# First-stage folds on VectorE in the front, and a new order of products and loads in odd steps

## The chip, the cores and the metric

The kernel runs on one core of a Trainium2 chip. The metric is the device time of one execution in microseconds (us). Before the change three timed runs gave 871.84, 869.36 and 871.62 us, median 871.62.

## What is computed

Two stages in one launch. The first is a causal long convolution by Fourier transform: x has 8 batches of 5696 tokens of 128 features, h is one filter of the same length for each feature. The second is a soft mixture of experts over all 45568 tokens: 32 slots, 8 experts.

```python
L = 2 * S                                  # S = 5696
Xf = np.fft.rfft(x, n=L, axis=1); Hf = np.fft.rfft(h, n=L, axis=0)
y = np.fft.irfft(Xf * Hf[None], n=L, axis=1)[:, :S, :]
x = y.reshape(B * S, D)
logits = x @ phi
d = softmax(logits, over tokens); slot_input = d.T @ x
slot_out[e] = relu(slot_input[e] @ w1[e]) @ w2[e]
c = softmax(logits, over slots); out = c @ slot_out
```

All data are float32.

## The kernel before

The transform is split in two factors, N1 = 90 and N2 = 64, and is done by matrix products with tables. There are nine groups of sequences: group 0 is h, groups 1 to 8 are the batches of x. The work is a pipeline of three parts.

- **A, the first stage.** A group is cut into NJ = 8 chunks, so there are NA = 72. `load_x(c)` (L184) fetches chunk c in two DMAs into one of three buffers xc. `fold(c, comp)` (L201, operation at L206) makes the sum (comp 0) and the difference (comp 1) of a chunk's two halves, the second half read backwards; each is one GpSimd operation of 128 x 512. The results lie in four buffers `xf`, two for even and two for odd chunks. `first_stage` (L210) multiplies them with the table s1 (L217), evicts two PSUM banks on ScalarE (L220) into a tile `fst` (four buffers) and stores that into f in DRAM (L226). `first_low(c)` makes the first 64 rows of the transform of one chunk; `first_high(c)`, in odd steps alone, makes the last 32 rows for the two chunks c-1 and c at once, and so reads all four `xf` buffers.
- **B, the spectrum.** `load_g` (L253) brings f back in twelve units per group (99 loads of 512 KB and 9 of 128 KB in all); `stage_b1` multiplies (L267) and, on VectorE, builds the filter's spectrum for group 0 (L285, L289) or multiplies with it (L285, L294); `stage_b2` transforms back (L309, evicted at L315) and stores into z in DRAM (L318).
- **C, the tokens.** `load_pair` (L346) brings z back into one buffer zc. `stage_c1` makes the last products (L365), with sums and differences on VectorE (L370, L371) and GpSimd (L384); `stage_c2` transposes (L393), `stage_c3` makes the logits (L402), `stage_c4`, `c5`, `softmax`, `dispatch` and `stage_c6` make both softmaxes and the running sum of slot inputs.

The order is written out by hand: the scheduler is switched off, and every engine works through its instructions in program order. A loop over steps t runs one letter after another of a string, `ORDER_E` when t is odd and `ORDER_O` when it is even (L577):

```python
ORDER_E, ORDER_O, XAHEAD = "xXYf1wb5s", "zPxXfb26db3m", 3
```

"x" is load_x(t + 3), "X" first_low(t), "Y" first_high(t), "f" both folds of chunk t + 1, "1" stage_c1 with stage_c4 in its middle, "w" what is left of stage_c1, "b" one unit of B, "z" load_pair, "P" load_g for the steps ahead. Part B lags by LAG_B = 9 steps, part C by 27. So steps 0 to 8 hold part A alone. All loads and stores of the loop are issued by SyncE (SP), one queue, in this same order: a load or store that has to wait holds up all behind it. After the loop comes a tail with its own order: the last token tiles, the experts (L767 to L788) and the output (L822 to L833).

Of the kernel before, what the change touches and what calls it, by code (L numbers as in the profile page):

```python
# [12 lines left out]
AL = mybir.AluOpType  # L13
# [64 lines left out]
def kernel(  # L78
# [24 lines left out]
    nc = tc.nc  # L103
# [3 lines left out]
    E, _, F = moe_w1.shape  # L107
# [16 lines left out]
    QP = HP // 2  # L124
# [18 lines left out]
    NT = B * NQ  # L143
# [52 lines left out]
                out=t_[X0 + r.start:X0 + r.stop, :, :, :].rearrange("p s n d -> p s (n d)"), in_=v)  # L196
        xs[c] = t_

    folded = {}

    def fold(c, comp):  # L201
        if c not in xs:
            return
        t_ = xs.pop(c) if comp else xs[c]
        y_ = xf[c % 2 * 2 + comp]
        nc.gpsimd.tensor_tensor(out=y_[:, :, :], in0=t_[:, 0, :, :], in1=t_[:, 1, ::-1, :],  # L206
                                op=AL.subtract if comp else AL.add)
        folded[(c, comp)] = y_

    def first_stage(tiles, width):  # L210

        st = apool.tile([P, CH, 2, D], F32, name="fst", tag="fst", bufs=4)
        for G in range(2):
            p = bank()
            for o, (c, comp) in enumerate(tiles):
                k = slice(0, HP) if width == HP else slice(HP, HP + QP)
                nc.tensor.matmul(p[o * width:(o + 1) * width, :], s1[:, comp + G, k],  # L217
                                 folded[(c, comp)][:, :, :].rearrange("p n d -> p (n d)"),
                                 start=True, stop=True)
            nc.scalar.activation(st[:, :, G, :],  # L220
                                 p[:, :].rearrange("p (n d) -> p n d", d=D), AF.Copy)
        for o, (c, comp) in enumerate(tiles):
            g, j = divmod(c, NJ)
            n0 = comp * HALF + CH * j
            k0, n = (0, N1A) if width == HP else (N1A, N1 - N1A)
            nc.sync.dma_start(  # L226
                out=fd[g].rearrange("q a r c d -> (q a) (r c d)")[k0:k0 + n, n0 * 2 * D:(n0 + CH) * 2 * D],
                in_=st[o * width:o * width + n, :, :, :].rearrange("k n c d -> k (n c d)"))
# [2 lines left out]
        first_stage([(c, comp) for comp in range(2)], HP)  # L231

    def first_high(c):

        both = [(c - 1 + i, comp) for i in range(2) for comp in range(2)]
        first_stage(both, QP)
        for b_ in both:
            del folded[b_]

    gs, prods = {}, {}  # L240

# [107 lines left out]
                                    a=2)[r:r + n, j * w_:(j + 1) * w_])  # L349
        zs[T] = t_  # L350

    def stage_c1(T, between):
        t_ = zs.pop(T)
        kr = used if t_ is zn else P
        y_ = ybufs.pop(0)
        ybufs.append(y_)

        def part(v, f):
            k = (2 * v + f) * CH
            return y_[:, k:k + CH, 0:D] if f == 0 else y_[:, k + CH - 1:k - 1:-1, 0:D]  # L360

        def product(o, tab, q):
            p = bank()
            for h_ in range(2):
                nc.tensor.matmul(p[h_ * HP:(h_ + 1) * HP, :], i1[0:kr, tab, :],  # L365
                                 t_[0:kr, h_, o, :, q, :], start=True, stop=True)
            return p[:, :].rearrange("p (n d) -> p n d", d=D)

        def fold_out(even, minus, plus):
            nc.vector.tensor_tensor(out=plus, in0=even, in1=minus, op=AL.add)  # L370
            nc.vector.tensor_tensor(out=minus, in0=even, in1=minus, op=AL.subtract)  # L371

        b_, a_ = product(0, 1, 1), product(0, 0, 0)
        nc.scalar.activation(part(0, 0), b_, AF.Copy)
        fold_out(a_, part(0, 0), part(1, 0))
        between()
        b_, a_ = product(1, 1, 0), product(1, 2, 1)
        nc.scalar.activation(om[:, :, :], b_, AF.Copy)

        def after():  # L380
            fold_out(a_, om[:, :, :], op[:, :, :])
            for v, o_, eng in ((1, op, nc.gpsimd), (0, om, nc.vector if tail else nc.gpsimd)):
                for part_, sign in ((part(v, 1), AL.subtract), (part(v, 0), AL.add)):
                    eng.tensor_tensor(out=part_, in0=part(v, 0), in1=o_[:, :, :], op=sign)  # L384

        ys[T] = y_
        return after

    def stage_c2(T):
        for k in (3, 1, 0, 2) if tail else (3, 2, 1, 0):  # L390
# [183 lines left out]
    for comp in range(2):  # L574
        fold(0, comp)
    wait_b2 = []
    ORDER_E, ORDER_O, XAHEAD = "xXYf1wb5s", "zPxXfb26db3m", 3  # L577

    for t in range(last_front + 1):
        us = list(units(t))  # L580

        def pair(lag):
            T, half = divmod(t - LAG_C - lag, 2)
            return T if half == 0 and 0 <= T < NT else None

        def prefetch(last):
            nonlocal loaded
            while loaded < len(queue) and queue[loaded][1] <= last:
                load_g(queue[loaded][0])
                loaded += 1  # L590

        def slot_b():
            fresh = bool(us)
            if fresh:
                u = us.pop(0)
                stage_b1(u, t < LAG_C or t >= NA)
                wait_b2.append(u)
            if len(wait_b2) > fresh:
                stage_b2(wait_b2.pop(0))

        T, U = pair(0), pair(2)
        after = []
        work_ = {
            "z": lambda: load_pair(pair(-1)) if pair(-1) is not None else None,
            "x": lambda: load_x(t + XAHEAD) if t < NA else None,
            "p": lambda: prefetch(t + 1) if t % NJ else None,
            "P": lambda: prefetch(t + 2),
            "q": lambda: prefetch(t + 1),
            "X": lambda: first_low(t) if t < NA else None,
            "Y": lambda: first_high(t) if t < NA and t % 2 else None,  # L610
            "f": lambda: [fold(t + 1, comp) for comp in range(2)] if t < NA else None,
            "d": lambda: dispatch(pair(3)) if pair(3) is not None else None,
            "b": lambda: slot_b(),
            "1": lambda: after.append(stage_c1(T, lambda: stage_c4(U) if U is not None else None))
            if T is not None else stage_c4(U) if U is not None else None,
            "w": lambda: [a_() for a_ in after],
            "2": lambda: stage_c2(pair(1)) if pair(1) is not None else None,
            "6": lambda: stage_c6(pair(5)) if pair(5) is not None else None,
            "5": lambda: stage_c5(U) if U is not None else None,
            "3": lambda: stage_c3(pair(1)) if pair(1) is not None else None,  # L620
            "m": lambda: column_max(pair(1)) if pair(1) is not None else None,
            "s": lambda: softmax(U) if U is not None else None,
            "g": lambda: prefetch(t + 1) if t % NJ == 0 else None,
        }
        if t == last_front:
            if pair(-1) is not None:
                load_pair(pair(-1))
            assert T is None and U is None
            if pair(3) is not None:
                dispatch(pair(3))  # L630
            slot_b()
            slot_b()
            slot_b()
            stage_c2(pair(1))
            slot_b()
            assert not us and not wait_b2
            V = pair(1)
            stage_c6(V - 2)
            stage_c3(V)
            column_max(V)  # L640
            break
        for c_ in (ORDER_E if t % 2 else ORDER_O):
            work_[c_]()
        assert not us
        if t == NA:
            lead.close()
            wts = inner.enter_context(tc.tile_pool(name="wts", bufs=1, side="right"))
            w1s = wts.tile([P, E, F], F32, name="w1s")
        if NA < t <= NA + E:
            nc.sync.dma_start(out=w1s[:, t - NA - 1, :], in_=moe_w1[t - NA - 1])  # L650
# [19 lines left out]
    tail["pool"] = cload.enter_context(tc.tile_pool(name="cload", bufs=2))  # L670
    y_ = tail["pool"].tile([P, Q * CH, D + 1], F32, name="y2", tag="y2", bufs=1)

    after = stage_c1(T, lambda: stage_c4(V))
    after()
    stage_c5(V)
    softmax(V)
    nc.gpsimd.memset(y_[:, :, D:D + 1], 1.0)
# [21 lines left out]
    for V in range(T, NT):  # L699
# [10 lines left out]
        N = T + 1 if V == T else V + 2  # L710
        after = None
        if N < NT:
            after = stage_c1(N, lambda: stage_c4(V))
            load_pair(N + 2)
        else:
            stage_c4(V)
        if after:
            after()
        if V > T:
            placed_c()  # L720
        stage_c5(V)
# [3 lines left out]
        softmax(V)  # L725
        if V == T:
            ybufs.insert(0, y_)
            stage_c1(T + 2, lambda: None)()
            load_pair(T + 4)
        else:  # L730
            for i in range(4 * (V - T - 1), min(4 * (V - T), E), 2):
                nc.sync.dma_start(
                    out=w2s[:, i:i + 2, :, :],
                    in_=moe_w2[i:i + 2].rearrange("e (p c) d -> p e c d", p=P))
    stage_c6(NT - 2)
    assert list(Ls) == [NT - 1] and not (ys or ds or prods or gs or zs or xs or folded or wait_b2
                or kept or landed)


# [129 lines left out]
```

## Time and profile before

| what | value |
|---|---|
| median of three runs | 871.62 us |
| the profiled execution's own time | 869.17 us |
| its span, first to last instruction | 867.4 us |
| granted TensorE clock, mean | 0.954 |
| TensorE busy (PE) | 770.7 us, 89% |
| VectorE busy (DVE) | 619.2 us, 71% |
| GpSimd busy (POOL) | 403.7 us, 47% |
| ScalarE busy (ACT) | 441.6 us, 51% |
| moved by DMA | 272.46 MB, mean 314 GB/s |
| folds, L206, on GpSimd | 144 of 1274 ns |

How to read the lines of the profile that follow. A group's line has the source line, the engine, the operation, the tiles as out<-in, and how many. In a timeline a line begins with the start and the length in us; the bracket at its end has the idle time of the engine ahead of it and what ended that. In the chain of waits a line has the start, the length and what the chain ran through. "SPq" is SP's queue of DMA issues. A stretch is a window of the span; its columns are the busy time of PE, PEld (weight loads, beside PE), DVE, ACT and POOL with counts, the granted clock, the mean busy share of the 16 DMA engines, and GB/s. A TensorE matmul of this kernel appears as two records, so the four matmuls of a low product appear as x8, the eight of a high product as x16.

### The profile page before, as it was taken

The numbers are of one execution on the slowest core, as the hardware profiler recorded it, in microseconds if no ns is written. First come the engines' busy times: TensorE is split into PE (matmuls) and PEld (weight loads), VectorE is DVE, ScalarE is ACT, GpSimd is POOL, SyncE is SP. The second block draws the span as 40 slices with busy tenths as digits, with TensorE's granted clock in tenths as the row PEclk, the third lists the DMA queues.
The fourth block names the chain that finished last, engine by engine and source line by source line (L and its number), as shares of the span: only waits on it lengthen the run. The fifth ranks groups of instructions, "written<-read, shape, count | busy, mean of one in ns | idle before, by whom it ended". The sixth has DMA issues, their size and how long they took to land.

```text
span 867.4 us, 20489 instructions
## 1 busy us (share of the span) xinstructions
PE 770.7 (89%) x7796; PEld 376.2 (43%) x7796; DVE 619.2 (71%) x928; ACT 441.6 (51%) x904; POOL 403.7 (47%) x385
## 2 busy tenths in 40 slices
PE   5888888888999999999999999999988879977893
PEld 1122333234444444444444444444444444444882
DVE  3059967667777878877888788877789995953552
ACT  2433344344555565556566556655544445773541
POOL 4453433245565555656555655556434432671000
PEclk9999999999999999999999999999999898989865
DMA  9899899999999999999999999999998986580898
GB/s 294 272 296 310 296 333 342 332 332 334 339 315 321 340 324 329 347 329 345 338 339 337 338 338 339 346 327 343 320 314 283 320 301 247 219 305 2 335 405 341
DMA packets 156109, 272.46 MB, mean 314 GB/s; under 512 B 12183, under 2 KB 113687, under 8 KB 152870
## 3 DMA queue, kind: packets, MB, share of 16 engines
q1 hardware_dynamic: 155435, 270.85, 90.2%
q8 instruction: 62, 1.02, 0.5%
q10 hardware_dynamic: 576, 0.31, 0.1%
q14 instruction: 36, 0.29, 0.1%
HBM read 142.81 MB, written 128.21 MB: 312 GB/s over the span
## 4 chain that ended last, share of the span: by engine, by line
PE 60%; DMA 15%; DVE 11%; SPq 3%; issue 2%; POOL 1%; ACT 1%; DVEq 0%; ACTq 0%
PE bank L217 14%; PE bank L365 13%; PE bank L309 7%; PE bt L267 7%; PE bank L393 6%; DMA zc<-z 6%; DMA out_dram<-o 3%; PE bank L478 3%; DVE yf L294 2%; DVE p L285 2%; DVE bt L285 2%; SPq L346 2%; DMA gt<-f 2%; PE op L822 2%; PE bank L402 2%
## 5 line engine op out<-in xcount | busy, mean ns | idle before, releaser
L206 POOL TENSOR_TENSOR x<-xc 128x512 f32<-128x512 f32 x144 | 180.0, 1274 | 229.5 <-PE bank L217 208.6
L217 PE MATMUL bank<-x,s 128*32 128x512 f32 (+1 forms) x1152 | 227.7, 613 | 16.0 <-DMA xc<-in_h_dram 8.1
L315 ACT ACTIVATE zst<-bank 128x512 f32<-128x512 f32 (+1 forms) x184 | 98.6, 586 | 190.9 <-PE bank L309 173.9
L220 ACT ACTIVATE fst<-bank 128x512 f32<-128x512 f32 x216 | 127.4, 598 | 109.5 <-PE bank L217 93.5
L285 DVE TENSOR_TENSOR p<-bt,Hi 128x1024 f32<-128x1024 f32 x96 | 111.4, 1160 | 33.7 <-PE bt L267 32.8
L309 PE MATMUL bank<-yf,vt 64*64 64x256 f32 x1440 | 103.1, 392 | 27.5 <-DVE yf L294 27.5
L365 PE MATMUL bank<-zc,i 128*64 128x512 f32 x480 | 115.8, 604 | 12.1 <-DMA zc<-z 8.2
L217 PEld LDWEIGHTS bank<-x,s 128*32 128x32 f32 (+1 forms) x1152 | 56.1, 124 | 155.5 <-issue 76.2
L294 DVE TENSOR_TENSOR yf<-bt,p 128x512 f32<-128x512 f32 x192 | 119.4, 663 | 3.3
L267 PE MATMUL bt<-gt,wt 64*64 64x256 f32 x1620 | 113.7, 388 | 5.8 <-DVE Hi L289 2.4
L285 DVE TENSOR_TENSOR bt<-bt,Hr 128x1024 f32<-128x1024 f32 x96 | 113.0, 1177 | 0.0
L267 PEld LDWEIGHTS bt<-gt,wt 64*64 64x64 f32 x1620 | 54.0, 132 | 80.6 <-issue 36.7
L309 PEld LDWEIGHTS bank<-yf,vt 64*64 64x64 f32 x1440 | 57.2, 136 | 58.9 <-issue 27.8
L384 POOL TENSOR_TENSOR y<-y,op 128x512 f32<-128x512 f32 x64 | 77.9, 1217 | 8.3 <-DVE op L370 5.2
L370 DVE TENSOR_TENSOR y<-bank,y 128x512 f32<-128x512 f32 x32 | 22.1, 691 | 72.8 <-PE bank L365 72.6
L393 PE MATMUL bank<-ident,y 109*128 109x109 f32 x512 | 64.3, 278 | 0.7 <-DVE y L384 0.7
L384 POOL TENSOR_TENSOR y<-y,om 128x512 f32<-128x512 f32 x54 | 64.0, 1185 | 2.1
L365 PEld LDWEIGHTS bank<-zc,i 128*64 128x64 f32 x480 | 30.5, 136 | 74.8 <-issue 47.1
L393 PEld LDWEIGHTS bank<-ident,y 109*128 109x128 f32 x512 | 54.3, 151 | 16.7 <-issue 11.1
L395 ACT ACTIVATE yt<-bank 128x360 f32<-128x360 f32 x128 | 51.4, 492 | 3.1 <-PE bank L393 3.1
L439 POOL MEMSET dt<- 64x8 f32 x32 | 3.4, 106 | 104.8 <-issue 70.7
L822 PE MATMUL op<-so,cT 32*128 32x128 f32 x704 | 45.6, 368 | 4.7 <-ACT o L831 4.3
(97 smaller groups left out, 824.6 us busy)
## 6 DMA issues: line engine op xcount, KB each, us to landing
gt<-f SPq DMA_DIRECT2D x99, 512.0 KB
z<-zst SPq DMA_DIRECT2D x88, 512.0 KB
f<-fst SPq DMA_DIRECT2D x144, 240.0 KB
zc<-z SPq DMA_DIRECT2D x30, 1024.0 KB
xc<-in_x_dram SPq DMA_DIRECT2D x64, 320.0 KB
f<-fst SPq DMA_DIRECT2D x144, 120.0 KB
out_dram<-o SPq DMA_DIRECT2D x16, 1024.0 KB
zc<-z SPq DMA_DIRECT2D x90, 128.0 KB
```

The source lines that it names most:

```text
L206: nc.gpsimd.tensor_tensor(out=y_[:, :, :], in0=t_[:, 0, :, :], in1=t_[:, 1, ::-1, :], op=AL.subtract if comp else AL.add)
L217: nc.tensor.matmul(p[o * width:(o + 1) * width, :], s1[:, comp + G, k], folded[(c, comp)][:, :, :].rearrange("p n d -> p (n d)"), start=Tr ...
L220: nc.scalar.activation(st[:, :, G, :], p[:, :].rearrange("p (n d) -> p n d", d=D), AF.Copy)
L267: nc.tensor.matmul(bt[q * HP:(q + 1) * HP, a, o, :], wt[r, 2 * i + q, :], t_[r, 2 * o + q, :, :].rearrange("p c d -> p (c d)"), start=True ...
L285: nc.vector.tensor_tensor(out=p_, in0=pv, in1=h_, op=AL.mult)
L294: eng.tensor_tensor(out=y_[r, 0:k, c, :], in0=pv[:, :, c, :], in1=pi[r, 0:k, 1 - c, :], op=op_)
L309: nc.tensor.matmul(bz[q][a * HP:(a + 1) * HP, o * 2 * D:(o + 1) * 2 * D], vt[r, i, a, :], y_[r, a * m + o, :, :].rearrange("p c d -> p (c ...
L315: nc.scalar.activation(st[:, 0:m, q, :], bz[q][:, 0:m * 2 * D].rearrange("p (o x) -> p o x", o=m), AF.Copy)
L365: nc.tensor.matmul(p[h_ * HP:(h_ + 1) * HP, :], i1[0:kr, tab, :], t_[0:kr, h_, o, :, q, :], start=True, stop=True)
L384: eng.tensor_tensor(out=part_, in0=part(v, 0), in1=o_[:, :, :], op=sign)
L393: nc.tensor.transpose(p[:, i * TR:(i + 1) * TR], ys[T][0:TR, k * CH + i, 0:D], ident[0:TR, 0:TR])
L822: nc.tensor.matmul(pq[q][:, k * D:(k + 1) * D], cT[rows, b, r0:r0 + RW, :] if k < n else cL[rows, :, :], so4[rows, :], start=True, stop=True)
```

## The change

Four edits, three of which alter what runs when.

1. The folds of the chunks 0 to 8 (c < LAG_B), which are those made ahead of the first B unit, go to VectorE. The others stay on GpSimd.
2. In odd steps the high product ("Y") comes first, then the folds of the next chunk ("f"), and then the low product ("X").
3. In odd steps the loads of x ("x") are issued after the stores of both products, not ahead of them.
4. `stage_c1` becomes a generator whose three pieces are "1", "j" and "w", with stage_c4 as a letter "4" of its own. The pieces come in the same order as before. `folded` becomes a function in place of a dictionary, which alters no instruction.

Even steps are as before.

```diff
-    folded = {}
+    def folded(c, comp):
+        return xf[c % 2 * 2 + comp]
...
         t_ = xs.pop(c) if comp else xs[c]
-        y_ = xf[c % 2 * 2 + comp]
-        nc.gpsimd.tensor_tensor(out=y_[:, :, :], in0=t_[:, 0, :, :], in1=t_[:, 1, ::-1, :],
-                                op=AL.subtract if comp else AL.add)
-        folded[(c, comp)] = y_
+        eng = nc.vector if c < LAG_B else nc.gpsimd
+        eng.tensor_tensor(out=folded(c, comp)[:, :, :], in0=t_[:, 0, :, :],
+                          in1=t_[:, 1, ::-1, :], op=AL.subtract if comp else AL.add)
...
-    def stage_c1(T, between):
+    def stage_c1(T):
...
         fold_out(a_, part(0, 0), part(1, 0))
-        between()
+        yield
         b_, a_ = product(1, 1, 0), product(1, 2, 1)
...
         ys[T] = y_
-        return after
+        yield
+        after()
+        yield
...
-    ORDER_E, ORDER_O, XAHEAD = "xXYf1wb5s", "zPxXfb26db3m", 3
+    ORDER_E, ORDER_O, XAHEAD = "YfXx14jwb5s", "zPxXfb26db3m", 3
...
-            "1": lambda: after.append(stage_c1(T, lambda: stage_c4(U) if U is not None else None))
-            if T is not None else stage_c4(U) if U is not None else None,
-            "w": lambda: [a_() for a_ in after],
+            "1": lambda: next(c1, None),
+            "4": lambda: stage_c4(U) if U is not None else None,
+            "j": lambda: next(c1, None),
+            "w": lambda: next(c1, None),
```

More of the change, by code (lines that the diff above doesn't have):

```diff
@@ L217, in first_stage @@
                 nc.tensor.matmul(p[o * width:(o + 1) * width, :], s1[:, comp + G, k],
-                                 folded[(c, comp)][:, :, :].rearrange("p n d -> p (n d)"),
+                                 folded(c, comp)[:, :, :].rearrange("p n d -> p (n d)"),
                                  start=True, stop=True)
@@ L233, in first_high @@
     def first_high(c):
[L235 to L238, printed above, removed]
+        first_stage([(c - 1 + i, comp) for i in range(2) for comp in range(2)], QP)
     gs, prods = {}, {}
@@ L601 @@
         T, U = pair(0), pair(2)
-        after = []
+        c1 = stage_c1(T) if T is not None else iter(())
         work_ = {
@@ L671 @@
     y_ = tail["pool"].tile([P, Q * CH, D + 1], F32, name="y2", tag="y2", bufs=1)
-    after = stage_c1(T, lambda: stage_c4(V))
-    after()
+    after = stage_c1(T)
+    next(after)
+    stage_c4(V)
+    next(after)
+    next(after)
     stage_c5(V)
@@ L712 @@
         if N < NT:
-            after = stage_c1(N, lambda: stage_c4(V))
+            after = stage_c1(N)
+            next(after)
+            stage_c4(V)
+            next(after)
             load_pair(N + 2)
@@ L717 @@
         if after:
-            after()
+            next(after)
         if V > T:
@@ L727 @@
             ybufs.insert(0, y_)
-            stage_c1(T + 2, lambda: None)()
+            for _ in stage_c1(T + 2):
+                pass
             load_pair(T + 4)
@@ L735 @@
     stage_c6(NT - 2)
-    assert list(Ls) == [NT - 1] and not (ys or ds or prods or gs or zs or xs or folded or wait_b2
+    assert list(Ls) == [NT - 1] and not (ys or ds or prods or gs or zs or xs or wait_b2
                 or kept or landed)
```

## The prediction

> **What bounds the kernel now.** I read the busy row by slices first, then the front of the kernel by stretches, then its timeline, and last the waits and the steady loop.
>
> The page shows three regimes. Each digit is the busy share of a fortieth of the span (21.7 us).
>
> ```profile
> PE   5888888888999999999999999999988879977893
> DVE  3059967667777878877888788877789995953552
> DMA  9899899999999999999999999999998986580898
> ```
>
> From slice 10 to 29 the tensor engine and the DMA engines are both at nine tenths or more: there, no rearrangement gains much. In the first two slices VectorE stands at 3 and 0, and DMA falls to 8. So the front has room. The stretch view cuts it at the pairs of first-stage steps (columns: PE, PEld, DVE, ACT, POOL busy, granted clock, DMA share, GB/s).
>
> ```profile
> 17.65:26.56 8.91, 7.17 (x33) 1.75 (x33) 0.00 (x0) 3.58 (x6) 4.95 (x5) 1.00 0.94 332
> 26.56:35.44 8.88, 7.15 (x33) 1.74 (x33) 0.00 (x0) 3.58 (x6) 4.92 (x5) 1.00 0.88 274
> 35.44:44.32 8.88, 7.15 (x33) 1.74 (x33) 0.00 (x0) 3.58 (x6) 4.92 (x5) 1.00 0.84 257
> 44.32:53.20 8.88, 8.17 (x48) 2.25 (x48) 0.34 (x1) 3.58 (x6) 4.92 (x5) 1.00 0.87 263
> ```
>
> A pair of steps takes 8.88 us there and nothing is full. The timeline says what sets that period.
>
> ```profile
> 25.24 4.92 POOL L206 TENSOR_TENSOR x<-xc 128x512 f32<-128x512 f32 x4 [3.96 <-PE bank L217]
> 26.56 7.45 PE L217 MATMUL bank<-x,s 128*64 128x512 f32 x32 [1.43 <-POOL x L206]
> ```
>
> It is a ring of two engines. GpSimd makes four folds (4.92 us) and then waits 3.96 us for the high product, because that is the last reader of the four fold buffers; TensorE in turn waits for the folds. 4.92 + 3.96 = 8.88: the period exactly. VectorE has no work in it at all (its first product comes at 52.86 us after 43.35 us idle).
>
> In the steady loop the same fold wait costs nothing. The chain of waits there is TensorE laid end to end; one pair of steps from 500.50 to 520.76 is 20.26 us, and 17 pairs from 234.34 to 581.10 average 20.40.
>
> ```profile
> 500.50 3.72 PE bank L217 x24
> 504.22 1.87 PE bank L365 x8
> ...
> 520.76 3.72 PE bank L217 x24
> ```
>
> [...] the trace has 691 ns for the sums of L370. [...] here 1274 ns (L206) over 691 is 1.84. [...] L384 on VectorE, both inputs in SBUF, takes 711 ns at best but 1552 ns in the median, beside L384 on GpSimd. [...] a load put behind a store in SP's queue inherits the store's wait. The trace shows such waits: SP before L226 for ACT fst, 14.0 us over 18.
>
> **The change part by part.**
>
> *Folds of chunks 0 to 8 on VectorE.* Eighteen folds leave GpSimd and go to VectorE; in the built program's instruction order they stand behind VectorE's start-up fills and ahead of its first product of the spectrum. Price of one: no such op (two SBUF inputs, GpSimd idle) is in the trace; the bounds are 0.69 (L370) and 1.55 us (L384 beside GpSimd). GpSimd has nothing else in the front, so I take 0.71, L384's minimum. Per pair: 4 x 0.71 = 2.8 us instead of 4.92. At the upper bound 4 x 1.55 = 6.2, still under 8.88.
>
> *The start.* VectorE fills zc, lt, dt and y until 9.6 us (zc 3.47 us from 4.89), where GpSimd folds from 6.83. So the first product moves from 8.15 to about 9.6 + 0.7 = 10.3: 2.2 us later. I cost it at nothing, because DMA is at 0.99 from 2.00 to 17.65 us, moving tables that the later stages need; if that cover is gone it costs up to 2.2.
>
> *High product first in odd steps.* The 24 matmuls stay 24 (3.72 us in the steady loop: 1.87 for the low ones, 1.85 for the high ones). But the even buffers come free after the high product, and the next even fold runs under the low one. The ring then is: high product, [fold | low product], [next fold | low product of the even step]. Each fold pair, 1.42 us, lies under a product of 1.87. The ring becomes TensorE's own 3.72 + 1.87 = 5.6 us per pair.
>
> *What is late next.* DMA: one pair needs share x length = 0.84 x 8.88 = 7.5 us to 0.88 x 8.88 = 7.8 us of all engines, over the 5.6 of TensorE. So the front becomes DMA-bound, and the gain isn't 8.88 - 5.6 but the idle DMA: 0.06 x 8.91 + (0.12 + 0.16 + 0.13) x 8.88 = 0.53 + 3.64 = 4.2 us. The first tenth of a full share is easy, the last is not: stretches that are called full stand at 0.96 to 1.02. I take 0.98, which leaves 0.02 x 35.5 = 0.7 us: a gain of 3.5 us. Bounds: 2.7 (0.96) and 4.2.
>
> *Does it last?* Behind the front lie the kernel's own spectrum products (52.86 to 98 us; VectorE 11.57 of 12 us, DMA 0.96 to 0.98) and then 120 to 165 us with DMA at 1.00 to 1.01. A gain that is DMA time passes through both; a gain that is only compute time would be eaten by the second. That is why I count DMA idle time and not the ring.
>
> *The spectrum's steps.* VectorE waits there for bt 0.91 + 0.71 + 0.23 + 1.28 = 3.1 us, behind products held up by folds on GpSimd. With the high product first, such a fold starts 1.87 us sooner. But DMA is near full; between 0 and 1.5, I take 0.4.
>
> *x loaded behind the stores.* In odd steps two loads go behind six stores in SP's queue, which wait for ACT's evictions. In the steady loop the loads are issued at 508.81 and the stores take 4.17 us after that; the loads' issue ends about 514.0. When a fold waited for its load, it began 5.7 to 7.1 us after the load's issue had ended (issue ended at 48.5, fold at 55.69; 73.3 and 80.31; 85.1 and 90.77). So it lands by 521.1. The fold is due when the high product ends, 520.76 + 1.87 = 522.6, and GpSimd's next work (L439) waits for ACT until 528.18: with 2.5 us of folds, it may begin at 525.6. Slack 1.5 us to the first point, 4.5 to the second. Cost: nothing, as long as that holds. The stores' earlier place helps only where a load waits for them, at the turn from one batch to the next (SP before L253 for DMA f<-fst, 2.8 us in all): 0 to 1, I take 0.
>
> *Steady loop otherwise.* Same products, same evictions, same four banks in turn: 0. The tail's stage_c1 is cut in pieces but runs in the same order: 0.
>
> **Sum:** 3.5 + 0.4 = 3.9 us off. Against the profiled execution's own 869.17 us (span 867.4) that gives 865.3. The median of the runs, 871.62, lies 2.5 above it, and the runs spread from 869.36 to 871.84. I start from the mean of all four, 870.5, and predict 866.6. A change under 0.3% (2.6 us) can't be told from none; "faster" means under 869.0.
>
> **The rivals.**
>
> *A, as above* (866.6; 50%).
>
> *B, compute time counts after all.* The front saves (8.88 - 5.6) x 3 = 10 us of ring, less 2.2 at the start; VectorE then begins the spectrum 7 to 8 us sooner, and the queue of transfers, now kept fuller, moves more per second (332 GB/s at 0.94 against 257 at 0.84). For it: VectorE at 0.96 of the spectrum's stretch. Against it: DMA is at 0.96 there too. 870.5 - 7.5 = 863 (15%).
>
> *C, the gain is hidden anyway.* TensorE and loads catch up in the DMA-full stretch from 120 us on; the DMA idle time only moves from the front to the spectrum's steps. For it: 12 x 0.13 = 1.6 us idle from 87 to 99 already. 870.5 - 0.5 = 870 (20%).
>
> *D, slower: the late x load.* If the load lands over 4.5 us later than I work out (latency above 11.5 us where 7 was seen), the fold, L447 and L384 behind it on GpSimd come late, and the transposes at L393, which follow L384's end (514.3) by half a microsecond, wait. The loop from 215 to 600 us has 19 pairs; 0.6 us each is 11.4, less A's 3.9: 870.5 + 7.5 = 878 (15%). For it: SP runs 8 us behind TensorE in the loop. Against it: the slack above.
>
> That the change doesn't do what it says is excluded: the instruction order shows the folds on VectorE and the products exchanged.
>
> **How the numbers follow.** A's own range is 864 to 869.5; B's is below, C's up to 872. The range 862 to 873 takes in A, C and most of B, and leaves out D and a little of B. Faster: three quarters of A, all of B, an eighth of C = 0.38 + 0.15 + 0.03 = 0.56. Slower: most of D = 0.13. Same: 0.31.
>
> **What would show it.** Folds on VectorE at about 0.71 us; DMA share 0.95 or more from 17 us to the first spectrum product; that product at 47 to 50 us instead of 52.86; the steady pair still 20.26 us. The prediction is wrong if the first spectrum product is early but the stretch at 165 us isn't (C), if GpSimd's folds wait for xc in the steady loop (D), or if VectorE's fold takes 1.5 us.

## The result and the profile after

The changed kernel takes 879.71 us (median of 20 runs, 874.86 to 892.77), the kernel before 872.04 us beside it (20 runs, 867.44 to 878.09). The ratio is 1.0093, with an interval of 1.0075 to 1.0112: **slower by 0.9%**, where 866.6 us was forecast. A ratio leaves out runs of more than 1.5% above the fastest of their kernel, here the one of 892.77 us, and so isn't quite the quotient of the medians. The profiled execution of the changed kernel took 877.15 us, its span is 875.4 us. Its mean granted TensorE clock is 0.952 against 0.954 before, so the clock doesn't make the difference.

The page's rows of busy tenths, of the kernel after (a digit is 21.9 us):

```profile
PE   5788787889999999899999998999988778977893
DVE  5259877567888888688888887878878995964542
DMA  8899999999999999999999999999999897670898
```

VectorE now works in the first slices (5 2 5 for 3 0 5), but the tensor engine (PE) shows 5 7 8 8 there for 5 8 8 8, and the DMA row is no fuller at its start (8 8 9 9 for 9 8 9 9). The front as a stretch view, of the kernel after (columns as in the prediction; the cuts are fixed ones, so that kernels can be laid side by side):

```profile
17.00:25.00 8.00, 7.45 (x44) 2.06 (x40) 2.58 (x4) 5.25 (x9) 0.00 (x0) 1.00 0.87 249
25.00:33.00 8.00, 6.09 (x32) 1.67 (x32) 2.50 (x4) 3.11 (x6) 0.00 (x0) 1.00 0.91 294
33.00:41.00 8.00, 6.24 (x34) 1.67 (x32) 2.50 (x4) 4.18 (x7) 0.00 (x0) 1.00 0.84 259
41.00:50.00 9.00, 6.73 (x30) 1.98 (x32) 1.29 (x2) 2.39 (x4) 3.41 (x3) 0.81 0.85 260
```

The same cuts of the kernel before:

```profile
17.00:25.00 8.00, 7.05 (x32) 1.74 (x32) 0.00 (x0) 2.99 (x5) 4.29 (x4) 1.00 0.95 339
25.00:33.00 8.00, 6.27 (x32) 1.65 (x32) 0.00 (x0) 2.98 (x5) 4.92 (x4) 1.00 0.88 271
33.00:41.00 8.00, 6.27 (x32) 1.46 (x26) 0.00 (x0) 2.98 (x5) 4.92 (x4) 1.00 0.81 251
41.00:50.00 9.00, 7.27 (x37) 1.86 (x40) 0.00 (x0) 3.63 (x7) 4.92 (x4) 1.00 0.86 261
```

GB/s times us is kilobytes: 8 x (249 + 294 + 259) + 9 x 260 = 8.76 MB after, 9.24 MB before. Between 17 and 50 us the DMA engines moved less, not more. VectorE's timeline there, of the kernel after, says what it waits for:

```profile
26.07 2.50 DVE L207 TENSOR_TENSOR x<-xc 128x512 f32<-128x512 f32 x4 [5.74 <-DMA xc<-in_h_dram]
33.31 2.50 DVE L207 TENSOR_TENSOR x<-xc 128x512 f32<-128x512 f32 x4 [4.74 <-DMA xc<-in_h_dram]
42.43 1.29 DVE L207 TENSOR_TENSOR x<-xc 128x512 f32<-128x512 f32 x2 [6.62 <-DMA xc<-in_x_dram]
53.68 1.23 DVE L281 TENSOR_TENSOR p<-bt,turn 128x1024 f32<-128x1024 f32 x1 [9.96 <-PE bt L263]
```

Four folds cost 2.50 us, as foretold, and the ring of two engines is gone: the bracket that named the high product now names the load. The first pair is shorter (26.07 to 33.31, 7.24 us), the next isn't (9.12 us), and the first spectrum product comes at 53.68 us, 0.8 us later than before.

In the steady loop, the chain of waits of the kernel after is no longer TensorE end to end:

```profile
520.02 1.82 PE bank L391 x16
521.84 0.39 PE bank L500 x4
522.22 0.03 SPq L342
...
524.02 7.80 DMA zc<-z
531.82 0.14 issue
531.95 3.43 PE bank L361 x8
```

A pair's token products wait for the load of zc, whose last issue ends at 523.97 us and whose data are there at 531.8. Not each pair does it; in the waits between 240 and 600 us, TensorE's wait for zc (total, times, longest) was in the kernel before

```profile
PE bank L365 <- DMA zc<-z: 2.5, 3, 1.4
```

and in the kernel after

```profile
PE bank L361 <- DMA zc<-z: 13.1, 8, 3.1
```

which is 10.6 us more. The stretch from 240 to 600 us as a whole, before:

```profile
240.00:600.00 360.00, 354.54 (x3660) 166.03 (x3663) 288.25 (x443) 210.76 (x437) 211.94 (x197) 1.00 0.97 335
```

and after:

```profile
240.00:600.00 360.00, 344.88 (x3527) 163.16 (x3529) 300.02 (x430) 204.87 (x424) 203.23 (x190) 0.99 0.97 326
```

TensorE is busy 9.7 us less. The DMA engines are as busy as before, 0.97, and **move 326 GB/s in place of 335**. A pair's bytes, 335 x 20.40 us = 6.83 MB, take 20.96 us at 326. (20.40 us is the mean of a pair of steps before.) The busy share doesn't show this loss; the bytes do.

### The profile page after: what moved, and what is told of

Its sections match the earlier page's. It is cut to its first block, busy times and chain, and to the rows that moved or that the text cites. A ratio compares the mean times of both kernels' runs of the same rounds, so it can differ in the third digit from the quotient of the medians.

```text
span 875.4 us, 20455 instructions
## 1 busy us (share of the span) xinstructions
PE 760.6 (87%) x7796; PEld 377.2 (43%) x7796; DVE 655.6 (75%) x946; ACT 441.1 (50%) x904; POOL 382.0 (44%) x367
## 4 chain that ended last, share of the span: by engine, by line
PE 51%; DMA 26%; DVE 12%; SPq 5%; issue 3%; ACT 1%; POOL 0%; DVEq 0%; ACTq 0%; POOLq 0%
PE bank L361 13%; DMA zc<-z 12%; PE bank L217 12%; PE bt L263 7%; PE bank L305 6%; PE bank L391 5%; DMA out_dram<-o 4%; DMA gt<-f 4%; SPq L342 3%; DVE p L281 3%; DVE bt L281 3%; DVE yf L290 2%; DMA f<-fst 2%; PE bank L476 2%; PE bank L429 2%
## 5 line engine op out<-in xcount | busy, mean ns | idle before, releaser
L207 POOL TENSOR_TENSOR x<-xc 128x512 f32<-128x512 f32 x126 | 158.1, 1276 | 207.9 <-PE bank L217 115.0
L217 PE MATMUL bank<-x,s 128*32 128x512 f32 (+1 forms) x1152 | 219.8, 621 | 17.2 <-DVE x L207 16.6
L220 ACT ACTIVATE fst<-bank 128x512 f32<-128x512 f32 x216 | 127.5, 598 | 103.1 <-PE bank L217 98.7
L361 PE MATMUL bank<-zc,i 128*64 128x512 f32 x480 | 118.4, 615 | 25.1 <-DMA zc<-z 21.6
L305 PE MATMUL bank<-yf,vt 64*64 64x256 f32 x1440 | 100.8, 385 | 24.8 <-DVE yf L290 24.3
L361 PEld LDWEIGHTS bank<-zc,i 128*64 128x64 f32 x480 | 32.4, 139 | 86.8 <-issue 63.0
```

What stands on the lines that cost most here:

```text
L207: eng.tensor_tensor(out=folded(c, comp)[:, :, :], in0=t_[:, 0, :, :], in1=t_[:, 1, ::-1, :], op=AL.subtract if comp else AL.add)
L220: nc.scalar.activation(st[:, :, G, :], p[:, :].rearrange("p (n d) -> p n d", d=D), AF.Copy)
L305: nc.tensor.matmul(bz[q][a * HP:(a + 1) * HP, o * 2 * D:(o + 1) * 2 * D], vt[r, i, a, :], y_[r, a * m + o, :, :].rearrange("p c d -> p (c ...
```

## The experiments

All kernels are made from the code of the changed one, in which "14jw" runs what "1w" ran before, so a diff is against `ORDER_E = "xXYf14jwb5s"` with folds on GpSimd (which is the kernel before), unless it says otherwise; the lines of a diff are cut to what matters. Each is compared with the kernel before on the same chip. The theories: 1, x is loaded late, as in rival D; 2, TensorE's shorter odd step outruns the transfers; 3, the folds on VectorE are the loss; 4, the order of transfers in SP's queue is. The transfers that SP issues in an odd step, in KB, are the key to all that follows:

| kernel | SP's transfers of an odd step, in order | ratio (interval) | median us (runs) |
|---|---|---|---|
| before | x 320, 36; low 240, 240; high 120 x4 | 1 | 870 to 872 |
| after | high 120 x4; low 240, 240; x 320, 36 | 1.0093 (1.0075 to 1.0112) | 879.71 (20) |
| folds_only | as before | 0.9963 (0.993 to 0.9995) | 867.82 (14) |
| high_first_only | x 320, 36; high 120 x4; low 240, 240 | 1.0173 (1.0132 to 1.0214) | 884.06 (6) |
| x_ahead_again | the same, folds on VectorE | 1.0145 (1.0105 to 1.0185) | 881.76 (6) |
| x_behind_only | low 240, 240; high 120 x4; x 320, 36 | 1.0143 (1.0105 to 1.018) | 882.81 (6) |
| stores_swapped | x 320, 36; high 120 x4; low 240, 240 | 1.0179 (1.0138 to 1.0219) | 886.48 (6) |
| high_first_low_stored_first | as before, products exchanged | 0.9988 (0.9968 to 1.0009) | 870.88 (22) |
| front_only | after's in steps 0 to 8, then before's | 1.0015 (0.9994 to 1.0037) | 872.68 (22) |
| loop_only | after's in steps 27 to 71 alone | 1.0077 (1.0039 to 1.0114) | 879.26 (9) |
| small_load_last | x 320; low 240, 240; high 120 x4; x 36 | 1.0023 (1.0002 to 1.0045) | 873.34 (22) |

**1. One part at a time.** Four kernels undo or keep one part.

```diff
folds_only:       +    eng = nc.vector if c < LAG_B else nc.gpsimd
high_first_only:  +    ORDER_E = "xYfX14jwb5s"
x_behind_only:    +    ORDER_E = "XYfx14jwb5s"
x_ahead_again:    +    ORDER_E = "xYfX14jwb5s"   (and the folds on VectorE)
```

> Folds of the first nine chunks on VectorE alone; products and loads in odd steps as before. Theory 1 (the late x load makes the loss): 868 to 871 us against 872 of before, since nothing is late. Theory 2 (the new order of the products makes the loss, because TensorE's odd step gets 0.25 us shorter and outruns the transfers): the same, 868 to 871. Theory 3 (the folds on VectorE make it, with their start 2.6 us later): 875 or more.

> High product first in odd steps alone; folds on GpSimd, x loaded ahead of the stores. Theory 1: 869 to 872, no loss. Theory 2: 878 to 882, the whole loss. Theory 3: 869 to 872.

> The x loads of odd steps behind the stores alone; low product first, folds on GpSimd. Theory 1: 878 to 884, the whole loss or more. Theory 2: 871 to 873. Theory 3: 871 to 873.

> The changed kernel with one thing undone: x loaded ahead of the stores again in odd steps. Theory 1: 866 to 869, the gain that the prediction worked out. Theory 2: 878 to 881. Theory 3: 876 to 880.

Measured: 867.82, 884.06, 882.81 and 881.76 us. The folds on VectorE are a gain of 0.4% (interval 0.05 to 0.7%), so theory 3 falls. The new order of products costs 1.7% with the loads of x where they were, and putting x ahead again in the changed kernel doesn't mend it: a late x load (theory 1) isn't the cause of that. Moving x alone costs 1.4%, which is what theory 1 had expected of it. But a late x must show as folds that wait for x, and in x_behind_only they wait no more than before: 15.6 us against 15.4 from 50 to 240 us, and not once for x from 240 to 600 us. Together the two moves cost less than the sum, 1.0093 with the folds' gain in it. The 884.06 and 881.76 us lie a little above what theory 2 gave. That left two readings of the products' part: TensorE's order, or the order of their stores in SP's queue.

**2. TensorE's order or the queue's.** The first two of the next four kernels split each product into its computation (X, Y) and its stores (k low, y high); the other two make the whole change in a part of the steps.

```diff
stores_swapped:               +    ORDER_E = "xXYykf14jwb5s"
high_first_low_stored_first:  +    ORDER_E = "xYfXky14jwb5s"
both:                         +    ORDER_O = "zPxXkfb26db3m"
front_only:  +    ORDER_E if 0 <= t < LAG_B else "xXYf14jwb5s"          (folds on VectorE)
loop_only:   +    ORDER_E if LAG_C <= t < NA else "xXYf14jwb5s"    (folds on GpSimd)
```

> Products in odd steps in the old order (low, then high), folds on GpSimd, x loaded ahead of the stores; only the stores are exchanged in SP's queue: the four small ones of the high product ahead of the two large ones of the low one. Theory 4 (the loop is bound by the transfers, and the order in which they are issued sets how much they move per second): 880 to 885, as with the high product first alone. Theory 2 (TensorE's shorter odd step): 870 to 873.

> The counterpart: the high product is made first in odd steps, but its stores are issued behind those of the low product, as before. Theory 4: 868 to 873, the loss gone. Theory 2: 880 to 885, the loss stays.

> The whole change in steps 0 to 8 alone (folds on VectorE, high product first, x behind the stores); from step 9 on the order of before. If the loss is made in the loop: 866 to 871. If the late x load in the front makes it: 876 to 880.

> The change of order from step 27 on alone, where all three parts run; folds on GpSimd and the old order in the front and in the steps of the spectrum. If the loss is made in the full loop: 877 to 882. If it is made by step 26: 870 to 873.

This pair decides. With TensorE, the folds and x as before and only the six stores exchanged, the loss is whole: 886.48 us, a little above theory 4's range. With the products exchanged and the stores in their old order it is nil: 870.88 us. The stretch from 240 to 600 us says the same in bytes; stores_swapped:

```profile
240.00:600.00 360.00, 347.87 (x3552) 160.88 (x3543) 278.97 (x431) 205.29 (x425) 202.50 (x188) 1.00 0.97 327
```

high_first_low_stored_first:

```profile
240.00:600.00 360.00, 352.83 (x3638) 168.25 (x3638) 310.21 (x442) 212.39 (x441) 212.38 (x198) 1.00 0.98 335
```

327 GB/s against 335. So the order of the stores in SP's queue makes the loss that comes with the products (theory 4), and theory 2 falls. It is also a matter of place: the whole change made in the loop alone costs 0.8%, and made in the front alone it gives nothing, 872.68 us where 866 to 871 was expected. 0.77 + 0.15 = 0.92 is near the 0.93 of the whole, but the intervals are 0.2 to 0.4 points wide on either side, so steps 9 to 26 may still add or take a little.

The front that gives nothing was to be the gain. Its cuts, of front_only:

```profile
17.00:25.00 8.00, 7.37 (x38) 2.08 (x34) 1.87 (x3) 4.74 (x8) 0.00 (x0) 1.00 0.92 302
25.00:33.00 8.00, 6.16 (x32) 1.67 (x32) 2.60 (x5) 3.62 (x7) 0.00 (x0) 1.00 0.91 292
33.00:41.00 8.00, 6.16 (x32) 1.67 (x32) 3.20 (x6) 3.58 (x6) 0.00 (x0) 1.00 0.92 299
41.00:50.00 9.00, 6.67 (x36) 2.05 (x40) 0.49 (x1) 3.58 (x6) 4.81 (x4) 1.00 0.79 262
```

Between 17 and 41 us the DMA share rises by 8 x (0.92 + 0.91 + 0.92 - 0.95 - 0.88 - 0.81) = 0.9 us, and in the next stretch 9 x (0.86 - 0.79) = 0.6 us of it goes back. By bytes front_only is ahead at first, 8 x (302 + 292 + 299) + 9 x 262 = 9.50 MB where the kernel before moves 9.24. But from 50 to 100 us it moves 302 GB/s where the kernel before moves 310, and that lead of 0.26 MB becomes a lag of 0.14. Idle DMA time moved; it hardly went.

**3. Why an order should matter: eight transfers at a time.** In the built program of the kernel after, SP's 868 issues take eight semaphores in turn, and 836 of the 860 behind the first eight carry a wait for the transfer eight places ahead, whatever its data. The waits in the traces show it as issues held by transfers that they have nothing to do with. Three of SP's waits in the kernel before, 240 to 600 us (total, times, longest):

```profile
SPq L195 <- DMA gt<-f: 21.0, 14, 2.1
SPq L226 <- DMA z<-zst: 19.6, 29, 1.0
SPq L195 <- DMA zc<-z: 19.4, 25, 3.1
```

and the three longest in the kernel after:

```profile
SPq L195 <- DMA zc<-z: 26.7, 21, 3.3
SPq L314 <- DMA gt<-f: 22.8, 17, 1.9
SPq L226 <- DMA gt<-f: 22.2, 14, 2.2
```

A load of x (L195) has no use for gt, but in the odd step of the kernel before gt stands eight places ahead of it; in the kernel after, the stores (L226) have that place. A pair of steps issues 24 transfers, three times round the eight. SP's timeline of the kernel after has them from one turn to the next (start, length, issues):

```profile
505.93 1.51 SPq L249 DMA_DIRECT2D gt<-f  x3
508.52 0.90 SPq L195 DMA_DIRECT2D xc<-in_x_dram  x2
509.52 0.78 SPq L226 DMA_DIRECT2D f<-fst  x2
510.40 0.38 SPq L314 DMA_DIRECT2D z<-zst  x1
511.65 0.35 SPq L511 DMA_DIRECT2D c_t<-cst  x1
513.11 0.36 SPq L314 DMA_DIRECT2D z<-zst  x1
515.25 3.96 SPq L226 DMA_DIRECT2D f<-fst  x6
519.41 1.65 SPq L195 DMA_DIRECT2D xc<-in_x_dram  x2
521.16 0.39 SPq L314 DMA_DIRECT2D z<-zst  x1
521.65 3.58 SPq L342 DMA_DIRECT2D zc<-z  x5
525.28 2.12 SPq L249 DMA_DIRECT2D gt<-f  x3
```

Counted from the first zc load of a turn, the third gt load is the 8th issue and the first of the six stores is the 16th: that is the wait of L226 for gt above. In the kernel before it is the first x load of the odd step that stands 16th.

A transfer of 36 KB takes one of the eight places, and so does one of 512 KB (theory 4a). The rival (4b) is that only what stands directly ahead of the zc load counts: small stores in the good orders, large ones or x in the bad ones.

```diff
small_load_last:       +    ORDER_E = "xXYhf14jwb5s"      ("x": rows 0 to 79 in odd steps, "h": the last 9 rows)
large_stores_halved:   +    cut = (0, n // 2, n)          (odd low stores: two of 30 rows, 120 KB, for one of 60)
folds_and_small_load_on_gpsimd:  +    (nc.sync if r.start == 0 else nc.gpsimd).dma_start(     (folds on VectorE)
folds_and_small_load_last:       small_load_last with the folds on VectorE
```

> The kernel before with one thing moved: in odd steps the second, 36 KB part of the x load is issued behind the stores, the 320 KB part stays ahead of them. The chunk is complete as late as with x behind the stores altogether. Theory 1 (a late x chunk holds up the fold and all behind it): 878 to 884. Theory 4a (only eight transfers are in flight, so small transfers early leave the DMA engines short of bytes) and theory 4b (what stands in the queue right ahead of the zc load makes that late): 866 to 873, no loss.

> The kernel before with the two 240 KB stores of odd steps each cut into two of 120 KB: the same bytes in the same place, eight small stores in a row, two more places taken among the eight in flight. Theory 4a: 879 to 887, a loss as large as that of the exchanged stores. Theory 4b: 870 to 874, since what stands ahead of the zc load is as before.

> The folds of the first nine chunks on VectorE, the order of before, and the 36 KB part of every x load issued from GpSimd's own queue, which frees two of SP's 24 issues in a pair of steps. Theory 4a: 858 to 866, better than the folds alone (868), as more bytes are in flight. Theory 4b: 866 to 870, like the folds alone. If GpSimd's issuing of transfers costs it much: 875 or more.

> The folds of the first nine chunks on VectorE together with the small load last in odd steps: the version that the runs so far point to. Theory 4a: 863 to 868. Theory 4b: 864 to 869. Theory 1: 875 or more.

Measured: 873.34, 907.02 (1.0386, 1.0345 to 1.0428), 866.42 (0.9894, 0.9837 to 0.9951; 6 runs) and 871.56 us (1.0009, 0.9989 to 1.003). Two more issues beside 24, for the same bytes, cost 907.02 - 871.45 = 35.6 us, over twice the most that 4a gave; 4b had no loss there, so what precedes zc can't be all. The last two kernels decide nothing between 4a and 4b: 866.42 us lies where their ranges meet, and 871.56 us is above both, so the small load last seems to take away the 0.4% that the folds alone give. In small_load_last a chunk of x is whole only behind all six stores, as in the changed kernel, and that costs 0.2% (interval 0.02 to 0.45%), not 1.4%: theory 1 falls here a second time. The stretch of large_stores_halved:

```profile
240.00:600.00 360.00, 335.54 (x3400) 155.63 (x3399) 266.74 (x413) 197.67 (x409) 193.23 (x179) 0.99 0.95 311
```

311 GB/s. The folds with the 36 KB loads on GpSimd's own queue, two of 24 issues fewer for SP, are the fastest kernel of the study. How much faster is less sure than the interval says: its six runs spread from 857.52 to 872.39 us, the ratio rests on four of them and gives 1.1%, and the medians of all runs give 0.6%.

**4. Rows, or places?** Halving by rows also leaves stores of 30 rows. The last four kernels try halves of all 60 rows (2 KB of each row), and take the 36 KB loads from SP in three orders.

```diff
large_stores_halved_by_columns:  +    cuts = (0, CH // 2, CH) if width == HP and halves else (0, CH)
small_load_on_gpsimd, swapped_..., changed_...:
                                 +    (nc.sync if r.start == 0 else nc.gpsimd).dma_start(
```

> As with the halved stores, but cut by columns: each large store of odd steps becomes two of 60 rows with 2 KB a row instead of two of 30 rows with 4 KB a row. Theory 4a (eight in flight, small ones waste places): a loss nearly as large as by rows, 890 to 910. Theory 4c (stores of 30 rows are slow): 872 to 880.

> The kernel before with the 36 KB part of every x load issued from GpSimd's queue; nothing else. Theory 4a: 862 to 868, most of the gain of the version with the folds. Theory 4c: 870 to 873.

> The exchanged stores (small ones ahead of the large ones, products in the old order), with the 36 KB part of every x load on GpSimd's queue. Theory 4a: 866 to 874, most of the 15 us of loss gone. Theory 4c: 880 to 886, the loss stays.

> The changed kernel as it is, with the 36 KB part of every x load on GpSimd's queue. Theory 4a: 864 to 872, faster than the kernel before or level with it. Theory 4c: 877 to 881.

| SP's order | all loads from SP | 36 KB loads from GpSimd |
|---|---|---|
| before | 1 | 1.0018 (0.9995 to 1.004) |
| before, folds on VectorE | 0.9963 (0.993 to 0.9995) | 0.9894 (0.9837 to 0.9951) |
| stores exchanged | 1.0179 (1.0138 to 1.0219) | 0.9998 (0.9972 to 1.0023) |
| the change | 1.0093 (1.0075 to 1.0112) | 1.0024 (0.9995 to 1.0054) |

Halving by columns takes 904.63 us (1.0369, 1.0322 to 1.0416), as by rows, so the count of rows doesn't make the loss (theory 4c falls). What the two kernels share is two more issues in a pair of steps, 26, which are no longer a whole number of turns of eight. With two issues fewer on SP, the exchanged stores cost nothing, as 4a had said. The changed kernel's loss shrinks to 0.2%, within its interval of none; its 873.92 us is between the ranges of 4a and 4c. And 4a had expected a gain for the old order too, where there is none: 870.79 us, which is what 4c gave.

**What stays open.** Shown are that the order in SP's queue makes the loss, that halving two stores costs 3.7 to 3.9%, and that taking two small loads from SP undoes the loss of the exchanged stores. How the order makes it is not shown. SP's waits for earlier transfers, added up from 240 to 600 us, don't tell good orders from bad: 125.4 us before, 117.7 in high_first_low_stored_first, but 134.9 in stores_swapped, 111.6 in the changed kernel and 97.0 in x_behind_only. Not separated is whether an issue costs by its place among eight or by SP's own time: the loss of large_stores_halved over its 36 odd steps is 35.6 / 36 = 0.99 us for two issues, 0.5 us each, and an issue of zc in the timeline above takes 3.58 / 5 = 0.7 us, an x load's 0.5 to 0.8. Adding two issues or taking two away also shifts which transfer waits for which. Nor is it settled whether freed places give anything beside the folds: to the old order alone they give nothing, and the interval of the kernel with both (0.9837 to 0.9951) overlaps that of the folds alone (0.993 to 0.9995). Nor is it explained why the exchange of stores (1.7 to 1.8%) and x behind them (1.4%) together cost 0.9 to 1.3%.

## Why the prediction was wrong, point by point

**The profile of before was read rightly.** The front was the ring described: with it broken, VectorE waits for loads and TensorE for the folds. The prices held: a fold on VectorE took 685 ns in the mean (L207, 18 of them) where 710 was taken; the first product began at 10.1 us where 10.3 was; TensorE's first-stage products of an odd step (x24 in the chain of waits) took 3.58 us where 3.72 stood. The folds alone gave 0.37% of 870.3 = 3.2 us; the 3.5 us of the forecast were for folds and products together.

**"What is late next" and "Does it last?" failed.** The step counted idle DMA time, 4.2 us of it, and said that such a gain passes through the full stretches. First, the idle time wasn't won. The first tenth of a full share, called easy, didn't come: the front waits for loads, but with x issued behind the stores DMA ran at 0.84 to 0.91, not at 0.98. With x ahead, x_ahead_again, it is idle later:

```profile
33.00:41.00 8.00, 7.62 (x36) 1.82 (x32) 2.59 (x4) 3.80 (x7) 0.20 (x1) 1.00 0.90 292
41.00:50.00 9.00, 4.82 (x20) 1.00 (x20) 0.00 (x0) 2.39 (x4) 4.77 (x4) 1.00 0.63 204
```

0.63 where the kernel before has 0.86: the front ended early and what follows it wasn't ready. The chain of waits of x_ahead_again says what that is:

```profile
43.22 3.83 DMA f<-fst
...
47.12 0.39 SPq L249
...
49.20 7.11 DMA xc<-in_x_dram
```

The first load of f (L249) has to wait until the front's last stores have landed, and the loads of x stand behind it in SP's queue. So the first spectrum product comes at 52.75 us there, 51.02 in front_only and 52.86 in the kernel before; 47 to 50 was the sign that the prediction had named. Here too the order of the stores counts: the waits of the loads of f for stores of f sum to 2.8 us in the kernel before and 8.2 in stores_swapped, and to 3.3 in high_first_low_stored_first and 8.6 in high_first_only; each pair differs in the order of the six stores alone. In the changed kernel they are 4.5 us. The prediction had this wait, at the turn of the batches, as a possible gain of 0 to 1. Second, the start of a step's low product, from one trace of each kernel, in us:

| kernel | step 8 | step 18 | step 44 | step 70 |
|---|---|---|---|---|
| before | 44.3 | 99.3 | 348.4 | 612.4 |
| after | 43.3 | 102.5 | 348.4 | 623.5 |
| front_only | 41.0 | 99.9 | 347.6 | 614.2 |
| x_ahead_again | 38.1 | 103.1 | 354.8 | 628.6 |
| folds_and_small_load_on_gpsimd | 39.8 | 96.0 | 342.9 | 611.4 |

3.3 us (front_only) and 6.2 us (x_ahead_again) of lead at step 8 are gone at step 18. The 0.4 us of gain expected in the spectrum's steps is a loss too: from step 8 to 18 the kernel before takes 55.0 us, the kernel after 59.2. That is rival C as written: the idle DMA time moves into the spectrum's steps. C gave 870; front_only, the part of the kernel of which it speaks, took 872.68 us.

**"Steady loop otherwise: 0" and "x loaded behind the stores: nothing" failed, and made the kernel slower.** The first listed products, evictions and banks and left out the stores, which the exchange of products takes along in SP's queue. That entry of zero stands for 1.8% if the stores are exchanged alone (stores_swapped, all odd steps), and for 0.8% if the whole change is made in the loop (loop_only). The prediction did let a load inherit the wait of a store ahead of it in SP's queue (SP before L226 for fst, 14.0 us over 18, in the trace of before). It left out the waits that the queue makes for its own earlier transfers, which stood in the same trace, 19 to 21 us from 240 to 600 us for each of the three kinds listed above.

The second asked only whether a fold gets its data in time. In the loop it does: in the changed kernel GpSimd's folds in the loop still wait for the high product, as this line of its waits from 240 to 600 us says:

```profile
POOL x L207 <- PE bank L217: 68.0, 17, 4.1
```

In the spectrum's steps it is late: from 50 to 240 us the folds wait 46.3 us for x, 15.4 before. That isn't the loss either, since high_first_low_stored_first has 43.3 us of it and loses nothing.

So rival D, which ended near the measured time (878 for 879.71), was right by luck; its mechanism, a fold of the loop that waits for x, isn't seen, and small_load_last and x_ahead_again speak against it. Moving x alone costs 1.4% with no longer wait of the folds; that this comes by SP's queue, as with the stores, is likely, and not shown by a kernel of its own.

**Where the time went.** The loss lies late: from step 44 to 70 the kernel before takes 264.0 us, the kernel after 275.1 (275.1 / 13 = 21.2 us for a pair of steps, where 20.26 was to stay), and the two are level at step 44. Of these 11.1 us, 3.1 are made up again by the end: the profiled executions differ by 8.0 us. What the waits show of the path is TensorE's wait for zc, 10.6 us more from 240 to 600 us. The other runs agree: in that stretch the seven other kernels with a loss of 0.7% or more wait 7.6 to 20.1 us for zc, and the nine without, 0.3 to 6.6. But the wait doesn't measure the loss: stores_swapped loses twice as much as the changed kernel with 7.6 us.

## What to carry to other kernels

When an edit changes the order of computation, write out what its DMA queue issues in that order, before and after, with the size of each: in this kernel, the order of six stores was worth 1.8% with every engine's work unchanged, and two more issues beside 24 nearly 4%. Where a trace shows issues that wait for transfers whose data they don't use (here 21.0 us of x loads behind gt, in the kernel before from 240 to 600 us), treat the queue itself as a resource, and try joining small transfers or giving them to another queue; here the latter undid a loss (1.0179 to 0.9998), but it gave the kernel before no gain (1.0018). Idle time of a resource is a gain only if what comes after it is ready to use it, so look for it in the next stretch too: here an early front was followed by a DMA share of 0.63 in place of 0.86.

## What the runs showed of the hardware that wasn't expected

A DMA share of 0.97 covers 326 as well as 335 GB/s, for the same transfers issued in another order: the engines show as busy and move 3% less. What they spend the time on isn't shown.

With the high product first, GpSimd's fold falls beside a tiny VectorE operation. In the kernel before, 240 to 600 us (count, busy, mean ns, idle):

```profile
L418 DVE SCALAR_TENSOR_TENSOR low<-mx,low 128x1 f32<-128x1 f32 x17 | 2.7, 160 | 0.6
```

and in the kernel after:

```profile
L416 DVE SCALAR_TENSOR_TENSOR low<-mx,low 128x1 f32<-128x1 f32 x17 | 19.8, 1166 | 0.6
```

One element per partition takes 1166 ns for 160. In all 17 cases of the kernel after a fold runs on GpSimd beside it (the one from 529.00 to 530.16 us beside the two folds from 527.64 to 530.14 us); in the kernel before, GpSimd runs nothing during any of the 17. Why it takes longer beside a fold isn't shown. It cost nothing here: high_first_low_stored_first has the same order on the engines, 1166 ns for this operation too, and no loss (0.9988). Issuing the 36 KB loads from GpSimd raised its busy time from 382.0 us (the changed kernel, with as many folds on GpSimd) to 421.8 us, by 0.55 us for each of the 72 loads, and that in the fastest kernel of all.
